# A first-layer product by seven block products instead of eight, beside an FFT convolution

## The chip, the cores and the metric

The kernel runs on one core of a Trainium2 chip, as one program. The time is the device time of an execution in microseconds (us); three executions of the kernel before took 1133.19, 1133.28 and 1133.93 us, median 1133.28.

An execution is worked on by TensorE (PE, matmuls, with PEld for the loading of their stationary operands), VectorE (DVE), ScalarE (ACT), GpSimd (POOL), SyncE (SP) and 16 DMA engines. Matmuls here write to tiles in PSUM, which the kernel divides into eight banks of 512 fp32 columns; the other operands lie in SBUF. Each engine works through its instructions in the order in which the built program has them, and waits on semaphores for the others.

## The reference

The input x has 2048 tokens of 576 channels. After a layer norm the result is the sum of three things: x itself, a state-space layer, and a dense layer.

```python
xn = (x - mean) / sqrt(var + 1e-5)
K  = real(sum over n of C[d,n] * exp(dt*A[d,n]*l) * dt*B[d,n])        # l = 0..2047, n = 0..127
y  = causal convolution of xn with K by FFT, + xn * Dskip
h  = silu(xn @ w1)            # w1: 576 x 4608
out = x + y + h @ w2          # w2: 4608 x 576
```

All inputs and the output are fp32.

## The kernel before, in words

**Precision.** The matmuls work in the type fp32r; the kernel's constants for it are cut to 12 bits of significand. Nearly every operand a is split into a high part (a cast on ScalarE, `gh`, `w1h`, `kh`) and a low part (a subtraction on VectorE, `gl`, `w1l`, `kl`), and a product is three matmuls: high x high, high x low, low x high.

**The dense layer** (`ffn`). The hidden 4608 features are 36 tiles of 128, in nine chunks of four (`FT`, `NCH`). The tokens are two halves of 1024, and each half two blocks of 512. For a block and a feature tile `up` (L276) writes a bank `ph` [128 features, 512 tokens]: 576 channels are four full slices of 128 and a rest of 64, so there are 3 x 4 matmuls for the slices and two for the rest, whose high and low parts lie one over the other in the 128 rows. That is 14 matmuls of 512 columns. SiLU, cast and subtraction (L292 to L294) make `gh` and `gl`. `down` (L296) then takes 128 tokens at a time, and for each half of the 576 output channels runs 12 matmuls of 288 columns into a bank `po` and adds it to `acc` on VectorE. The main loop (L343) goes over half, chunk and block; it puts the next block's four `up` between the four `down` of the present one. `load_w1` fetches the w1 columns of two feature tiles at once, `split_w1` and `split_w2` make high and low parts.

**The convolution** runs beside it. First come layer norm and transposes; then a generator (`kgen`) builds K in tables on VectorE and ScalarE, a first FFT stage (`kp`, `z` on TensorE, `spread` for the input) writes `d1k` and `d1u` to DRAM; then 32 rounds of the spectral stage (`spectral`, L632) load a slab of each (`kr`, `ur`), split it (`kh`, `kl`, `uh`, `ul`), transform it with the matrices `mm` (`pk`, `pu`), multiply (copies `ka`, `kb` by ScalarE out of `pk`, three products on VectorE and a sum `y`), split `y` (`yh`, `yl`), transform back (`pb`) and write the copy `yo` to `d2`. Round k+1's front stands ahead of round k's `pb`. At the end `tail` loads `d2` again (`ys`, L724) and `add_conv` (L731) adds the last transform `py` to the output rows: for the first token half into rows read back from DRAM (`r0`), for the second into `acc`.

**What sets the order.** `weave` (L31) advances the generator of the dense layer, and at each of its 288 steps lets the side generator go on as far as the step it names; `marks` and `tail_at` (L755) are such places as shares of all steps. A scheduler then moves instructions among the engines' queues by its own estimates; `tc.high_priority` and `behind` (an issue order between two instructions) steer it. PSUM: pool `ps1` has two banks (`ph`), `ps2` three (`po`), `pss` three for all side work.

## Time and profile before

| | |
|---|---|
| median of three executions | 1133.28 us (1133.19 to 1133.93) |
| span of the profiled execution, first to last instruction | 1133.7 us |
| its own time as a run | not listed; the slowest of the three is 0.2 us above its span, the median 0.4 below |
| TensorE busy | 1112.3 us, 9184 matmuls |
| VectorE busy | 916.6 us |
| ScalarE busy | 711.7 us |
| granted TensorE clock, mean | 0.997 |
| spectral stage, first to last `pb` | 697.2 to 1018.9 us |

How to read the rows that follow. Slices: the span in 40 equal parts, one digit each, the busy share in tenths. Windows: a stretch, its length, then the busy time and the number of instructions of each engine. Groups: line, engine, operation, output and inputs by the program's names (with shape), how many, then busy time in all, mean nanoseconds of one, and the idle time of the engine just before, with what ended it. Timeline: start, duration, engine, line, operation. An end of a matmul is modelled, and matmuls overlap: the distance between starts tells what one costs.

### The profile page before, as it was taken

How to read it: one execution, taken by the hardware profiler on the slowest of the kernel's cores; microseconds unless marked ns; L12 is line 12 of the kernel's file. 1: busy time of each engine (PE TensorE's matmuls, PEld its weight loads, DVE VectorE, ACT ScalarE, POOL GpSimd, SP SyncE). 2: the span in 40 equal slices, each digit the busy share in tenths (PEclk: the TensorE clock that was granted, in tenths of full speed). 3: DMA queues.
4: the chain of work that ended last, by engine and by line, in shares of the span. 5: the costliest groups of instructions: out<-in, count | busy, mean ns of one | idle time of the engine just before them, and what ended most of it. 6: DMA issues, size and time to landing. Idle time of an engine off the chain costs nothing.

```text
span 1133.7 us, 22905 instructions
## 1 busy us (share of the span) xinstructions
PE 1112.3 (98%) x9184; PEld 1002.8 (88%) x9184; DVE 916.6 (81%) x1540; ACT 711.7 (63%) x1235; POOL 74.4 (7%) x130
## 2 busy tenths in 40 slices
PE   6999999999999999999989999999999999999998
...
DVE  6699898999999999999979838787777778763433
ACT  4665456666767676667666647777777877752211
...
GB/s 271 136 158 201 146 34 82 82 92 103 91 97 65 137 69 119 53 163 169 263 116 103 77 160 143 155 178 125 159 131 151 150 136 184 82 101 193 231 174 56
DMA packets 160458, 151.24 MB, mean 133 GB/s; under 512 B 87216, under 2 KB 127168, under 8 KB 159712
## 3 DMA queue, kind: packets, MB, share of 16 engines
...
q10 hardware_dynamic: 384, 0.89, 0.3%
...
## 4 chain that ended last, share of the span: by engine, by line
PE 81%; DVE 11%; DMA 3%; ACT 2%; issue 2%; POOL 0%; SPq 0%; ACTq 0%; DVEq 0%
PE po L309 35%; PE ph L284 28%; PE kp L598 3%; PE ph L286 2%; PE ph L285 2%; PE pk L721 2%; PE pu L721 2%; PE pb L721 2%; PE z L613 1%; PE py L741 1%; DMA dxt<-xt 1%; DVE gl L294 1%; DVE S L577 1%; DMA w2r<-in_B_w_dram 1%; DVE w2l L273 1%
## 5 line engine op out<-in xcount | busy, mean ns | idle before, releaser
L309 PE MATMUL po<-w2h,gh 128*128 128x288 f32 x1152 | 339.1, 298 | 6.3 <-ACT gh L293 3.2
L309 PE MATMUL po<-w2l,gh 128*128 128x288 f32 x1152 | 338.0, 295 | 0.0
L309 PE MATMUL po<-w2h,gl 128*128 128x288 f32 x1152 | 334.6, 296 | 0.5 <-DVE gl L294 0.4
L309 PEld LDWEIGHTS po<-w2h,gh 128*128 128x128 f32 x1152 | 215.8, 188 | 18.2 <-issue 4.2
L309 PEld LDWEIGHTS po<-w2l,gh 128*128 128x128 f32 x1152 | 216.3, 188 | 4.3
L309 PEld LDWEIGHTS po<-w2h,gl 128*128 128x128 f32 x1152 | 215.1, 188 | 3.4 <-DVE gl L294 1.0
L284 PE MATMUL ph<-xh,w1h 128*128 128x512 f32 (+1 forms) x592 | 162.1, 390 | 0.7 <-ACT xh L122 0.7
L284 PE MATMUL ph<-xl,w1h 128*128 128x512 f32 (+1 forms) x592 | 162.2, 390 | 0.0
L284 PE MATMUL ph<-xh,w1l 128*128 128x512 f32 (+1 forms) x592 | 161.7, 387 | 0.0
L313 DVE TENSOR_TENSOR acc<-po,acc 128x288 f32<-128x288 f32 x288 | 126.5, 452 | 37.2 <-PE po L309 35.5
L292 ACT ACTIVATE gf<-ph 128x512 f32<-128x512 f32 (+1 forms) x148 | 86.8, 587 | 104.0 <-PE ph L286 94.9
L294 DVE TENSOR_TENSOR gl<-gf,gh 128x512 fp32r<-128x512 f32 (+1 forms) x148 | 99.4, 673 | 48.4 <-ACT gh L293 47.8
L284 PEld LDWEIGHTS ph<-xl,w1h 128*128 128x128 f32 x592 | 109.5, 191 | 21.5 <-issue 0.4
L284 PEld LDWEIGHTS ph<-xh,w1l 128*128 128x128 f32 x592 | 108.7, 190 | 19.9
L284 PEld LDWEIGHTS ph<-xh,w1h 128*128 128x128 f32 x592 | 104.8, 190 | 18.6 <-issue 2.3
L293 ACT CAST gh<-gf 128x512 fp32r<-128x512 f32 (+1 forms) x148 | 89.9, 609 | 17.9 <-PE po L309 15.2
L557 ACT ACTIVATE c<-th,magic 128x1040 f32<-128x1040 f32 x36 | 42.1, 1169 | 52.4 <-DVE C L578 30.1
L271 ACT CAST w2h<-w2r 128x576 fp32r<-128x576 f32 x72 | 47.2, 673 | 29.6 <-DMA w2r<-in_B_w_dram 17.4
L559 ACT ACTIVATE c<-th 128x1040 f32<-128x1040 f32 x36 | 38.7, 1074 | 36.0 <-DVE th L558 36.0
L273 DVE TENSOR_TENSOR w2l<-w2r,w2h 128x576 fp32r<-128x576 f32 x72 | 53.6, 752 | 6.2 <-ACT w2h L271 6.1
L255 DVE TENSOR_TENSOR w1l<-w1r,w1h 128x640 fp32r<-128x640 f32 x72 | 56.9, 820 | 1.0 <-ACT w1h L253 0.8
L577 DVE TENSOR_TENSOR S<-th,C 128x1024 f32<-128x1024 f32 x36 | 43.9, 1220 | 16.8 <-ACT th L560 16.8
...
## 6 DMA issues: line engine op xcount, KB each, us to landing
w2r<-in_B_w_dram SPq DMA_DIRECT2D x72, 288.0 KB, 3.3
w1r<-in_B_w_dram SPq DMA_DIRECT2D x35, 512.0 KB, 3.8
d1u<-u POOLq DMA_DIRECT2D x32, 288.0 KB, 2.7
d1k<-stage SPq DMA_DIRECT2D x18, 512.0 KB, 6.8
ur<-d1u SPq DMA_DIRECT2D x32, 288.0 KB, 3.9
kr<-d1k SPq DMA_DIRECT2D x32, 288.0 KB, 2.7
d<-yo POOLq DMA_DIRECT2D x32, 288.0 KB, 3.9
ys<-d SPq DMA_DIRECT2D x32, 288.0 KB, 9.2
```

The costliest lines, as they stand in the source:

```text
L255: pins["w1l"] = nc.vector.tensor_sub(l1, src, h1).ins
L271: pins["w2h"] = nc.scalar.copy(h2, r2).ins
L273: nc.vector.tensor_sub(l2, r2, h2)
L284: nc.tensor.matmul(ph, w[:, kt, :], v[:, kt, a:e], start=n + kt == 0, stop=False)
L292: nc.scalar.activation(gf, ph, AF.Silu)
L293: pins["gh"] = nc.scalar.copy(gh, gf).ins
L294: pins["gl"] = nc.vector.tensor_sub(gl, gf, gh).ins
L309: pins["pe"] = nc.tensor.matmul(po[:, :HD], G[blk, t][g][:, js], W2[half, c, t][w][:, hs], start=n == 0, stop=n == 3 * FT - 1).ins
L313: nc.vector.tensor_add(acc[j][:, hs], po[:, :HD], acc[j][:, hs])
L557: nc.scalar.activation(c65, th, AF.Identity, bias=magic)
L577: nc.vector.tensor_mul(ov3, t[:, :, 0:64].rearrange("n d (x y) -> n d x y", y=32), mv3)
L721: nc.tensor.matmul(dst, st, mv[:, hs], start=n == 0, stop=n == 3 * len(terms) - 1)
```

## The change

Seven of the nine chunks in the second token half (`WINO_C = 2` and on) compute the first product in another way. Take a pair of feature tiles (256 features), the two blocks of the half (1024 tokens) and the 512 channels of the full slices: w1 is a 2 x 2 matrix of blocks (two feature tiles, two halves of 256 channels), x likewise (two halves of channels, two blocks of tokens). Strassen's method in Winograd's form needs seven block products instead of eight, of sums of blocks. The rest of 64 channels is added as before.

- `wino_x` makes the sums of x once per half (S1 to S4, from the high and low parts), and `d4`, a difference for the rest of the channels.
- `sums` makes the sums of w1 for each pair on VectorE; `prep` and `split` make the high and low parts of what is used: `c1` and `c2` from w1 itself, `t13` and `t24` from the sums.
- Per pair, `wino_ffn` runs the products into four banks: `pb` (from `ps2`), in which three of them and a last one build up, `pf` (from `pss`), and the two `ps1` banks, `pa` and `pc`, which are held all the time. A copy of `pb` into `pa` and one of `pf` to SBUF (`f5`) are made by ScalarE; `pc` = `pb` + `f5` and `f5` = `pb` + `f5` are sums on VectorE, written where the next product goes on adding. `gate` is SiLU and the split; for `f5` it reads SBUF.
- `down` takes a list of terms: blocks of one pair or of two pairs in a row, always four rows of 128 tokens at a time.
- To make room, the pool of the spectral stage (`kl`) has one buffer of everything but the matrices, of which there are two of one round each (before: two of two rounds each); `y2` goes and `kb` is written over; the tail has four `ys` and two `r0` buffers, and loads a row's `ys` behind the `add_conv` four rows earlier. The dense layer has 276 steps, and the marks are counted anew.

The diff, cut to its core:

```diff
@@ -64,6 +64,7 @@
     nc = tc.nc
     FT = 4
     NCH = NFT // FT
+    WINO_C = 2
...
@@ -293,21 +295,22 @@
                 pins["gh"] = nc.scalar.copy(gh, gf).ins
                 pins["gl"] = nc.vector.tensor_sub(gl, gf, gh).ins
 
-        def down(blk, jj):
+        def down(blk, jj, terms=None):
             half, c, b = blk
             j = 8 * half + 4 * b + jj
             js = slice(jj * P, (jj + 1) * P)
             if half == 1 and c == NCH - 1:
+                add_conv(j, acc[j])
                 conv_load(j + AHEAD)
-                add_conv(j, acc[j])
+            terms = terms or [(G[blk, t], W2[half, c, t]) for t in range(FT)]
             for h in range(2):
                 hs = slice(h * HD, (h + 1) * HD)
                 po = ps2.tile([P, 512], F32, tag="ps2", name="po")
                 n = 0
-                for t in range(FT):
+                for gs, ws in terms:
                     for g, w in ((0, 0), (0, 1), (1, 0)):
-                        pins["pe"] = nc.tensor.matmul(po[:, :HD], G[blk, t][g][:, js], W2[half, c, t][w][:, hs],
-                                                      start=n == 0, stop=n == 3 * FT - 1).ins
+                        pins["pe"] = nc.tensor.matmul(po[:, :HD], gs[g][:, js], ws[w][:, hs],
+                                                      start=n == 0, stop=n == 3 * len(terms) - 1).ins
                         n += 1
...
-        for i, blk in enumerate(blocks):
+        plain = blocks[:2 * (NCH + WINO_C)]
+        for i, blk in enumerate(plain[:-1]):
             half, c, b = blk
-            later = i + 1 < len(blocks)
+            later = True
             new = (half, c + 1) if c + 1 < NCH else (half + 1, 0)
-            more = new[0] < 2
+            more = new < (1, WINO_C)
...
+                if new == (1, WINO_C) and (b, step) == (0, "u2"):
+                    load_w1(1, WINO_C, 0)
+        yield from wino_ffn(load_w1, load_w2, split_w2, R1, W2, plain[-1], down)
+
+    def wino_ffn(load_w1, load_w2, split_w2, R1, W2, before, down):
+
+        ps_a = ps1.tile([P, 512], F32, tag="ps1", name="pa")
+        ps_c = ps1.tile([P, 512], F32, tag="ps1", name="pc")
+        A, A22, S1, S2, S3, S4, x40, x41, d4 = wino["x"]
+        for t in (ps_a, ps_c):
+            nc.tensor.matmul(t, x40[:, :P], x40, start=True, stop=True)
+        G, WT = {}, {}
+
+        def split(src, name, n):
+            h = wp.tile([P, 5, P], F32R, tag="w1h", name="w1h", bufs=FT + 1)
+            l = wp.tile([P, 5, P], F32R, tag="w1l", name="w1l", bufs=FT + 1)
+            k = src.shape[1]
+            with behind(pins["gh"]):
+                nc.scalar.copy(h[:, :k], src)
+            nc.vector.tensor_sub(l[:, :k], src, h[:, :k])
+            WT[name, n] = h, l
+
+        def raw(n):
+            return R1[1, n // 2, n % 2 * 2]
+
+        def sums(n):
+            r1 = raw(n)
+            tr = [wino["pool"].tile([P, 4, P], F32, tag="tr", name="tr", bufs=2) for _ in range(2)]
+            nc.vector.tensor_sub(tr[0].rearrange("p (l k) f -> p l k f", l=2),
+                                 r1[:, 0:4, P:2 * P].rearrange("p (l k) f -> p l k f", l=2),
+                                 r1[:, 0:2, :].rearrange("p k (l f) -> p l k f", l=2))
+            nc.vector.tensor_add(tr[1][:, 0:2], tr[0][:, 2:4], r1[:, 0:2, 0:P])
+            nc.vector.tensor_sub(tr[1][:, 2:4], r1[:, 2:4, 0:P], tr[1][:, 0:2])
+            WT["raw", n] = tr
+
+        def prep(n, part):
+            if n >= NFT // 2:
+                return
+            r1 = raw(n)
+            if part == "c1":
+                split(r1[:, 0:5, 0:P], "c1", n)
+            elif part == "c2":
+                split(r1[:, 2:5, P:2 * P], "c2", n)
+            elif part == "t13":
+                split(WT["raw", n][0], "t13", n)
+            elif part == "t24":
+                split(WT["raw", n][1], "t24", n)
+
...
+        def prod(dst, w, x, start=False, stop=False):
+            (wh, wl), (xh, xl) = w, x
+            n = 0
+            for a, v in ((wh, xh), (wh, xl), (wl, xh)):
+                for kt in range(2):
+                    pins["pe"] = nc.tensor.matmul(dst, a[:, kt], v[:, kt], start=start and n == 0, stop=stop and n == 5,
+                                                  skip_group_check=True).ins
+                    n += 1
+
+        def rest(dst, name, n, at, x4, stop=True):
+            for i in range(2):
+                pins["pe"] = nc.tensor.matmul(dst, WT[name, n][i][:, at], x4, start=False, stop=stop and i == 1,
+                                              skip_group_check=True).ins
+
...
+        first, end = WINO_C * FT // 2, NFT // 2
+
...
+        def downs(n):
+
+            if n < first:
+                return [lambda jj=jj: down(before, jj) for jj in range(4)]
+            b = 1 - n % 2
+            if n == first:
+                ns = (n,)
+            else:
+                ns = (n - 1, n)
+            return run_of(b, ns)
+
+        def run_of(b, ns):
+            fs = [2 * n + i for n in ns for i in range(2)]
+            blk = (1, NCH - 1 if ns[-1] == end - 1 else WINO_C, b)
+            return [lambda jj=jj: down(blk, jj, [(G[b, f], W2[1, f // FT, f % FT]) for f in fs]) for jj in range(4)]
+
+        for n in range(first, end):
+            d = downs(n - 1)
+            pb = ps2.tile([P, 512], F32, tag="ps2", name="pb2")
+            pf = pss.tile([P, 512], F32, tag="pss", name="pf")
+            f5 = wino["pool"].tile([P, 512], F32, tag="f5", name="f5", bufs=1)
+            prod(pb, unit("c1", n, 0), A[0], start=True)
+            with tc.high_priority():
+                nc.scalar.copy(ps_a, pb)
+            prod(pf, unit("t13", n, 0), S1, start=True)
+            rest(pf, "c2", n, 2, x41)
+            with tc.high_priority():
+                nc.scalar.copy(f5, pf)
+            yield 0
+            d[0]()
+            second(n, 0, "split")
+            second(n, 1, "split")
+            yield 0
+            prod(pb, unit("t24", n, 0), S2)
+            with tc.high_priority():
+                nc.vector.tensor_add(ps_c, pb, f5)
+            d[1]()
+            second(n + 1, 0, "load")
+            second(n + 1, 1, "load")
+            if n + 1 < end:
+                sums(n + 1)
+            prep(n + 1, "c1")
+            yield 0
+            prod(pb, unit("t13", n, 2), S3)
+            with tc.high_priority():
+                nc.vector.tensor_add(f5, pb, f5)
+            d[2]()
+            prep(n + 1, "t13")
+            yield 0
+            d[3]()
+            yield 0
+            gate(f5, 1, 2 * n + 1)
+            prod(ps_c, unit("c2", n, 0), S4)
+            rest(ps_c, "c2", n, 2, d4)
+            gate(ps_c, 0, 2 * n + 1)
+            prep(n + 1, "c2")
+            prod(ps_a, unit("c1", n, 2), A[1])
+            rest(ps_a, "c1", n, 4, x40)
+            gate(ps_a, 0, 2 * n)
+            yield 0
+            prod(pb, unit("t24", n, 2), A22)
+            rest(pb, "c1", n, 4, x41)
+            gate(pb, 1, 2 * n)
+            prep(n + 1, "t24")
+            load(n + 2)
+            yield 0
+        b = 1 - (end - 1) % 2
+        for f in run_of(b, (end - 2, end - 1)):
+            f()
+            yield 0
+        for k, f in enumerate(run_of(1 - b, (end - 1,))):
+            f()
+            if k % 2:
+                yield 0
+
+    def wino_x(sx, xp):
+
+        (ah, al, x40), (bh, bl, x41) = xts[2], xts[3]
+
...
+        e = sx.tile([P, 512], F32, name="e4")
+        e2 = sx.tile([P, 512], F32, name="e42")
+        d4 = xp.tile([P, 512], F32R, name="d4")
+        x21, x22 = join(bh, bl, 0, "x21"), join(bh, bl, 2, "x22")
+        nc.vector.tensor_add(x22, x21, x22)
+        S1 = parts(x22, *new("s1"))
+        x11 = join(ah, al, 0, "x11")
+        nc.vector.tensor_sub(x21, x11, x21)
+        nc.vector.tensor_sub(x11, x22, x11)
+        S2 = parts(x11, *new("s2"))
+        x12 = join(ah, al, 2, "x12")
+        nc.vector.tensor_sub(x12, x12, x11)
+        S4 = parts(x12, *new("s4"))
+        nc.vector.tensor_sub(e, x40.bitcast(F32), x41.bitcast(F32))
+        nc.scalar.copy(e2[:64], e[64:])
+        nc.vector.tensor_add(e[:64], e[:64], e2[:64])
+        nc.scalar.copy(d4[:64], e[:64])
+        nc.vector.tensor_sub(d4[64:], e[:64], d4[:64])
+        yield 0
+        S3 = parts(x21, bh[:, 0:2], bl[:, 0:2])
+        wino["x"] = ([(ah[:, 0:2], al[:, 0:2]), (ah[:, 2:4], al[:, 2:4])], (bh[:, 2:4], bl[:, 2:4]),
+                     S1, S2, S3, S4, x40, x41, d4)
+        wino["pool"] = xp
 
     kl = yp = pa = tail_at = None
     kf = {}
@@ -631,16 +845,12 @@
 
     def spectral():
         def front(k):
-            if k % 2 == 0:
-                mm = kl.tile([P, 2, 4, P], F32R, tag="mm", name="mm")
-                nc.gpsimd.dma_start(mm, cm23[:, k:k + 2])
-                mats.append(mm)
-            mk = mats[-1][:, k % 2]
+            mk = kl.tile([P, 4, P], F32R, tag="mm", name="mm", bufs=2)
+            nc.gpsimd.dma_start(mk, cm23[:, k])
             us, ks = load_split(d1u[k * P:(k + 1) * P, :], "u"), load_split(d1k[k * P:(k + 1) * P, :], "k")
             ka = kl.tile([P, D], F32, tag="ka", name="ka")
-            kb = kl.tile([P, D], F32, tag="kb", name="kb", bufs=1)
-            y = kl.tile([P, D], F32, tag="y", name="y", bufs=1)
-            y2 = kl.tile([P, D], F32, tag="y2", name="y2", bufs=1)
+            kb = kl.tile([P, D], F32, tag="kb", name="kb")
+            y = kl.tile([P, D], F32, tag="y", name="y")
             for h in range(2):
                 hs = slice(h * HD, (h + 1) * HD)
                 pk = pss.tile([P, 512], F32, tag="pss", name="pk")
@@ -652,12 +862,11 @@
                 pu = pss.tile([P, 512], F32, tag="pss", name="pu2")
                 mm3(pu[:, :HD], [(mk[:, 0], mk[:, 1], us)], hs)
                 nc.vector.tensor_mul(y[:, hs], pu[:, :HD], ka[:, hs])
-                nc.vector.tensor_mul(y2[:64, hs], pu[64:, :HD], kb[:64, hs])
-                nc.vector.tensor_mul(y2[64:, hs], pu[:64, :HD], kb[64:, hs])
-            nc.vector.tensor_add(y, y, y2)
+                nc.vector.tensor_mul(kb[:64, hs], pu[64:, :HD], kb[:64, hs])
+                nc.vector.tensor_mul(kb[64:, hs], pu[:64, :HD], kb[64:, hs])
+            nc.vector.tensor_add(y, y, kb)
             return mk, split_of(y, "y")
 
-        mats = []
         nxt = front(0)
         for k in range(32):
             mk, ys = nxt
@@ -672,25 +881,25 @@
             nc.gpsimd.dma_start(d2.rearrange("(p k) d -> k p d", k=32)[k], yo)
             yield 1 + (k + 1) / 32
 
-    AHEAD = 6
+    AHEAD = 4
 
...
         def load_r0(j):
-            r0s[j] = yp.tile([P, 2, D], F32, tag="r0", name="r0", bufs=4)
+            r0s[j] = yp.tile([P, 2, D], F32, tag="r0", name="r0", bufs=2)
             nc.sync.dma_start(r0s[j], dr0[j * P:(j + 2) * P, :].rearrange("(i p) d -> p i d", p=P))
 
         def last(j):
-            conv_load(j + AHEAD, 8)
             add_conv(j, r0s[j - j % 2][:, j % 2, :])
+            conv_load(j + AHEAD)
             if j % 2:
                 store(r0s[j - 1], j - 1, (nc.gpsimd,))
 
         steps, at = [], tail_at[0]
         for j in range(8):
-            for f in (conv_load, load_r0)[:2 - j % 2]:
+            for f in (conv_load, load_r0)[j >= AHEAD:2 - j % 2]:
                 steps.append((at, f, j))
                 at += tail_at[1]
...
-    def conv_load(j, first=0):
-        if first <= j < NJ:
-            yss[j] = yp.tile([P, 4, HD], F32, tag="ys", name="ys", bufs=AHEAD + 2)
+    def conv_load(j):
+        if j < NJ:
+            yss[j] = yp.tile([P, 4, HD], F32, tag="ys", name="ys", bufs=AHEAD)
...
-        marks = (0.13, 0.595, 0.822)
-        tail_at = (0.895, 0.0045, 0.922, 0.005)
+        marks = (0.1357, 0.613, 0.855)
+        tail_at = (0.895, 0.0055, 0.919, 0.0052)
...
+        xp = ctx.enter_context(tc.tile_pool(name="xp", bufs=1))
+        with tc.tile_pool(name="sx", bufs=1) as sx:
+            for _ in wino_x(sx, xp):
+                yield 0.6215
+        with tc.tile_pool(name="kl", bufs=1) as kl:
             for at in spectral():
-                yield marks[1] + (at - 1) * (marks[2] - marks[1])
+                yield 0.6215 + (at - 1) * (marks[2] - 0.6215)
...
-    weave(fg, 2 * NCH * 2 * (FT + 4), sd)
+    weave(fg, 276, sd)
```

38 lines of the change are left out of this document (37 added, 1 removed).

## The prediction, made before the changed kernel had run

> **What bounds the kernel now.** I read the page first: span, busy shares, slices.
>
> ```profile
> span 1133.7 us, 22905 instructions
> PE 1112.3 (98%) x9184; PEld 1002.8 (88%) x9184; DVE 916.6 (81%) x1540; ACT 711.7 (63%) x1235; POOL 74.4 (7%) x130
> PE   6999999999999999999989999999999999999998
> DVE  6699898999999999999979838787777778763433
> ACT  4665456666767676667666647777777877752211
> ```
>
> TensorE is the bound nearly everywhere. VectorE is as full as TensorE in slices 7 to 20 (the generator of the convolution kernel) and at 70 to 80% in slices 24 to 35 (the spectral stage); both side engines are light in the last 100 us. A busy share hides pauses between matmuls, so next come two stages by windows, and the timeline for the distance from one matmul to the next.
>
> ```profile
> 200.00:500.00 300.00, 299.47 (x3165) 270.21 (x3164) 289.33 (x426) 205.16 (x310) 11.38 (x21) 1.00 0.37 94
> ...
> 1020.00:1134.00 114.00, 109.35 (x831) 89.24 (x829) 42.88 (x88) 22.59 (x38) 11.27 (x23) 1.00 0.64 163
> ```
> ```profile
> 660.00:1010.00 350.00, 349.97 (x2198) 324.25 (x2197) 268.74 (x488) 263.22 (x546) 25.89 (x47) 1.00 0.49 148
> ```
> ```profile
> 889.80 0.39 PE L285 MATMUL ph<-x,w1h 128*128 128x512 f32 x1
> 890.03 0.40 PE L286 MATMUL ph<-x,w1l 128*128 128x512 f32 x1
> ...
> 901.17 0.29 PE L309 MATMUL po<-w2l,gh 128*128 128x288 f32 x1
> 901.30 0.29 PE L721 MATMUL pu<-uh,mm 128*128 128x288 f32 x1
> ```
>
> Columns of the windows after the length: TensorE, weight load, VectorE, ScalarE, GpSimd, granted clock, DMA share, GB/s. A 512-wide matmul costs 0.23 us (0.227 in runs of them), a 288-wide one 0.13. In the spectral stage VectorE has 81 us to spare of 350 and ScalarE 87; TensorE has none.
>
> **The change, part by part.** *TensorE.* Call the two feature tiles of one first-weight load a pair; 14 pairs change. A pair had four outputs of 14 matmuls, 56; it gets seven products of 6 and four remainders of 2, 50. So 84 matmuls of 512 go, 2 come (they set up the two held banks): 82 x 0.227 = 18.6 us less. The down products, the spectral matmuls and the tail keep their number.
>
> *What the products cost elsewhere.* The durations come from the rows of the spectral stage and two of the whole span:
>
> ```profile
> L313 DVE TENSOR_TENSOR acc<-po,acc 128x288 f32<-128x288 f32 x84 | 37.6, 454 | 2.0 <-PE po L309 1.0
> L294 DVE TENSOR_TENSOR gl<-gf,gh 128x512 fp32r<-128x512 f32 x44 | 30.3, 690 | 20.0 <-ACT gh L293 19.6
> ...
> L654 DVE TENSOR_TENSOR y<-pu,ka 128x288 f32<-128x288 f32 x63 | 28.6, 454 | 12.0 <-ACT ka L649 8.9 <-PE pu L721 2.1
> ...
> L708 DVE TENSOR_TENSOR kl<-kr,kh 128x576 fp32r<-128x576 f32 x32 | 24.2, 758 | 31.4 <-ACT kh L707 31.3
> ...
> L657 DVE TENSOR_TENSOR y<-y,y 128x576 f32<-128x576 f32 x31 | 23.3, 752 | 0.0
> L255 DVE TENSOR_TENSOR w1l<-w1r,w1h 128x640 fp32r<-128x640 f32 x24 | 19.1, 821 | 0.2
> L273 DVE TENSOR_TENSOR w2l<-w2r,w2h 128x576 fp32r<-128x576 f32 x21 | 15.6, 753 | 0.1
> ```
> ```profile
> L293 ACT CAST gh<-gf 128x512 fp32r<-128x512 f32 x44 | 27.3, 620 | 0.9
> L292 ACT ACTIVATE gf<-ph 128x512 f32<-128x512 f32 x44 | 26.4, 599 | 12.3 <-PE ph L286 11.9
> L650 ACT ACTIVATE kb<-pk 64x288 f32<-64x288 f32 x64 | 26.1, 408 | 1.4 <-DVE y L656 0.3
> ...
> L648 ACT COPY ka<-pk 64x288 f32<-64x288 f32 x64 | 25.1, 392 | 11.6 <-PE pk L721 10.6
> ...
> L671 ACT COPY yo<-pb 128x288 f32<-128x288 f32 x60 | 23.1, 399 | 7.4 <-PE pb L721 6.4
> L707 ACT CAST kh<-kr 128x576 fp32r<-128x576 f32 x32 | 21.6, 674 | 1.9 <-DMA kr<-d1k 1.0
> ...
> L253 ACT CAST w1h<-w1r 128x640 fp32r<-128x640 f32 x24 | 16.2, 724 | 0.0
> L271 ACT CAST w2h<-w2r 128x576 fp32r<-128x576 f32 x21 | 13.7, 671 | 0.5 <-DMA w2r<-in_B_w_dram 0.2 <-PE po L309 0.2
> L621 ACT COPY stage<-z 128x512 f32<-128x512 f32 x2 | 1.1, 635 | 3.9 <-PE z L613 3.9
> ```
> ```profile
> L577 DVE TENSOR_TENSOR S<-th,C 128x1024 f32<-128x1024 f32 x36 | 43.9, 1220 | 16.8 <-ACT th L560 16.8
> ...
> L294 DVE TENSOR_TENSOR gl<-gf,gh 128x256 fp32r<-128x256 f32 x8 | 3.3, 415 | 2.2 <-ACT gh L293 2.2
> ```
>
> VectorE, per pair: splits 0.82 + 0.55 (384 wide, between the rows) + 2 x 0.69 in place of 2 x 0.82, +1.1; weight sums 0.69 + 2 x 0.42 = 1.5; two sums of products 1.4. That is 4.0, and 56 over 14 pairs. Once: a dozen 1024-wide operations on the tokens, 14.6 and some 2 for the small ones; 8 more additions into acc, 3.6. Together 76 us. ScalarE: per pair +1.0 of splits and two 512-wide copies, 1.2, and 4 casts once: some 37 us. Eleven VectorE rows of the stage (L313 to L273) sum to 283.7 where the window has 268.7 busy, thirteen ScalarE rows (L293 to L621) to 273.4 against 263.2, since one row overlaps the next: factors 0.947 and 0.963.
>
> *Where it lands.* The built order of the changed kernel, weighed with these rows, packs the spectral stage tighter: from its first to its last pb product TensorE has 277.6 us of matmuls instead of 321.5, VectorE 294 of row time instead of 266, ScalarE 273 instead of 255. With the factors that is 278, 278 and 263: three full engines. The order repeats every seven spectral rounds (two pairs); row time per round:
>
> ```
> round       1     2     3     4     5     6     7    sum
> TensorE    7.4   6.8   8.6  11.1  14.2   9.2   7.8  65.1
> VectorE    5.7   9.7  11.4   7.7  10.3  13.9   8.3  67.0
> ScalarE    6.0  10.8  10.5   6.6   8.5  12.8   6.7  61.9
> ```
>
> In rounds 1 to 3 ScalarE needs 27.3 x 0.963 = 26.3 us where TensorE has 22.8; in 4 to 7 TensorE has 42.3 and the others less. TensorE runs in order, so what it loses in the first three it does not get back. The least loss is 26.3 - 22.8 - 1.6 (ScalarE's copies of the next round can be that far ahead) = 1.9 per seven rounds. I walked the order by hand for more, from pb of round 1 at 0, with 0.40 for ka and kb copies, 0.65 for 576-wide operations and 0.1 for a hand-over: eight copies until 1.3, two casts and yo to 3.35, y sum on VectorE 3.4, yh 4.15, copy of pf 4.75, yl 4.95, sum into pc 5.6; only then may product t13 x S3 start, at 5.7 where the order has 3.7. ScalarE then works without a break from 4.75 to 13.55 and waits for product c1 x A1, ends its SiLU at 15.6, yh 16.25, copy of pb 16.85, gh 17.45, then ka and kb of the next round to 19.65. Only that frees the bank (three in this pool) for the second pu: 19.75 against 13.7. Later sums in the same seven add up to 2.5. I take 6.0; ends 1.9 and 8.5. There are 31/7 = 4.43 such groups: 26.6 us (8.4 to 37.7).
>
> *The start of the stage.*
>
> ```profile
> L598 PE MATMUL kp<-S x1152: 219/219/219, 169.3 to 655.6; 128*32 128x64 f32 x192
> ```
> ```profile
> L721 PE MATMUL pb<-yh,mm x128: 288/294/302, 697.2 to 1018.9; 128*128 128x288 f32 x128
> ...
> L708 DVE TENSOR_TENSOR yl<-y,yh x32: 747/759/761, 693.8 to 1014.4; 128x576 fp32r<-128x576 f32 x32
> ```
>
> Between the generator's last table and the first yl VectorE had 23 us of row time and 38 us of clock; it now has 39.2 x 0.947 = 37.1, and yl itself, 0.8, before pb may use it. The order gives TensorE 33.5 from the last kp to that pb: 4.4 late, with one hand-over 4.7 (2 to 8).
>
> *Smaller things.* The pair's pb holds one of three banks of the down products, two where pairs meet; an evacuation of 0.45 then stands between two halves in some places: 0 to 8 us over 14 pairs, I take 2, near the low end, since 0.45 is what the row shows per place. Buffers of one in the spectral stage: kr is reloaded behind kl, 2.7 us and 1.4 of casting, inside every round. mm is loaded per round, 16 more issues on GpSimd, which is 7% busy.
>
> ```profile
> mm<-in_cm_dram POOLq DMA_DIRECT2D x16, 512.0 KB, 4.3
> ...
> kr<-d1k SPq DMA_DIRECT2D x32, 288.0 KB, 2.7
> ```
>
> The tail's conv loads go from six ahead to four, issued behind add_conv instead of ahead of it. Their first py now stands 60 us of matmuls behind the last pb instead of 17, so I cost them at nothing. On SP's queue the loads of the last two rows stand behind the store of rows 8 and 9, which waits for the down product of row 9; the order leaves them 8.5 us from there to their py.
>
> ```profile
> DMA to landing us min/median/max: 4.0/9.2/13.0
> ```
>
> The lower end held when few loads were under way, as then; without that cover the end is up to 4 us later (0 to 4, I take 0). The moved marks are steps counted anew (276 for 288); the generator keeps its place.
>
> *Sum.* Against the profiled execution, span 1133.7, some 0.4 over the median of 1133.28 and 0.2 under the slowest run: 1133.7 - 18.6 + 26.6 + 4.7 + 2.0 - 0.4 = 1148.0.
>
> **A rule weighed.** TensorE's idle of 3.15 us was followed by a slow stretch:
>
> ```profile
> 575.00:580.00 5.00, 2.45 (x14) 1.98 (x12) 1.73 (x2) 4.09 (x6) 0.00 (x0) 1.00 0.76 224
> 580.00:585.00 5.00, 4.24 (x19) 4.01 (x20) 5.00 (x8) 4.14 (x10) 0.54 (x1) 0.66 0.00 1
> ```
> ```profile
> 580.60 0.40 PE L309 MATMUL po<-w2h,gh 128*128 128x288 f32 x1 [3.15 <-ACT gh L293]
> ```
>
> 5 x (1 - 0.66) = 1.7 us were lost beside the idle itself. My walk has one idle of 4 us per seven rounds (15.7 to 19.75); if each were followed by that loss, 4.43 x 1.7 = 7.5 more, 1155.5. The Trainium skill, TensorE: Matmul & The Clock Gate, "Why this matters for your kernels", warns of idle gaps over about 3 us between bursts of matmuls, which put the array back to half rate; by that rule the time would be this 1155.5, and the row agrees with it once.
>
> **Rivals.** *The gain survives:* ScalarE keeps just its least loss, 8.4, and the start costs 2: 1133.3 - 18.6 + 8.4 + 2 = 1125. It decides if the loss of a group is under 3 us. For it: VectorE ran 289 of 300 us in the generator while TensorE lost 0.5. Against it: there TensorE waited for no chain through ScalarE. At the best 1115. *The matrix load sets the rounds:* mm of round k+2 overwrites that of k, so its load starts behind pb of k, and the order has the first pk of k+2 just 1.8, 1.8, 2.5, 5.0, 5.9, 3.2 and 4.6 us later. With 4.4 for a load that is 8.3 per group; if half comes on top, 1148 + 18 = 1166, if all, 1185. Against it: half the bytes, and pk waits for kl as late. *The clock gate* above: 1155.5. That the matmuls do not go away is excluded by the order.
>
> **Chances.** Two tenths of a per cent, about what a measurement tells here, is 2.3 us. Forecast without the clock loss 0.35 and with it 0.17, matrix load 0.13: slower 0.65. Gain survives 0.31. In between 0.04. The likeliest case alone has 1133.3 - 18.6 + (8.4 to 37.7) + (2 to 8) + (0 to 8), in practice 1137 to 1160; the range, to leave out a tenth on each side, is 1121 to 1170.
>
> **What would show it.** Right: the products and remainders together 700 matmuls where the pairs had 784; idle TensorE in the spectral stage of some 27 us, ended by ScalarE (ka, kb) and VectorE in the first rounds of each seven, with VectorE over 90% there; about 5 us before the first pb; nothing in the last 100 us. Wrong: a spectral stage without TensorE idle (then 1115 to 1125), pk waiting for mm above all, or a new wait for ys in the tail.

## The result: 1204 us, and the profile after

The changed kernel takes 1204.01 us (four runs, 1201.54 to 1205.23) where the kernel before takes 1133.61 (four runs, 1133.19 to 1134.53): a ratio of 1.0612, 95% interval 1.0595 to 1.0628. The forecast was 1148; the direction came out, the loss is 70 us where 14 were forecast. The profiled execution took 1201.54 us with a span of 1199.8, 66.1 more than the span before.

The page of the changed kernel, its busy shares and slices:

```profile
span 1199.8 us, 23093 instructions
PE 1126.0 (94%) x9102; PEld 993.5 (83%) x9102; DVE 984.0 (82%) x1661; ACT 739.9 (62%) x1297; POOL 81.2 (7%) x146
PE   6999999999999999999999878979889898999898
DVE  6799999999999999999995868878788788746444
ACT  4665556666666776766764368687677876634120
PEclk9999999999999999999999879999999999999899
```

The matmuls did go away: 9102 for 9184. But TensorE pauses from slice 23 on, and over a slice neither VectorE nor ScalarE is full there (no digit over 8). The same in windows (length, TensorE, weight load, VectorE, ScalarE, GpSimd, granted clock, DMA share, GB/s), first the start of the stage, the spectral stage and the rest of the changed kernel, then the stage of the kernel before:

```profile
640.00:706.00 66.00, 54.99 (x415) 46.30 (x413) 44.19 (x69) 27.45 (x48) 2.01 (x3) 0.87 0.29 74
706.00:1044.00 338.00, 299.96 (x1772) 261.81 (x1772) 273.32 (x507) 253.29 (x539) 33.12 (x61) 0.99 0.45 134
1044.00:1199.00 155.00, 147.81 (x1054) 123.74 (x1052) 74.79 (x147) 41.21 (x72) 11.22 (x23) 0.97 0.51 136
```
```profile
698.00:1019.00 321.00, 321.00 (x2037) 298.92 (x2037) 251.60 (x459) 241.12 (x505) 24.43 (x45) 1.00 0.46 140
```

TensorE, which never paused in the stage before, is idle for 38 of 338 us now, 11 of the 66 before it, 7 behind it. The clock, 1.00 before, is 0.87, 0.99 and 0.97: 66 x 0.13 + 338 x 0.01 + 155 x 0.03 = 17 us at the most. That counts slow time in which TensorE stood still as well. Four stretches in which the clock is 0.50 (671.74 to 678.57, 695.63 to 709.28, 798.03 to 801.44 and 1118.88 to 1125.71 us) hold 24.8 us of TensorE's work; half of that, 12.4 us, is what the clock cost, where the kernel before lost 3.3 in the same way. Three rows of groups give the places by which I cut the time (last table product `kp`, first and last `pb` of the rounds, last `py`):

```profile
L812 PE MATMUL kp<-S x1152: 219/219/219, 168.1 to 650.9; 128*32 128x64 f32 x192
L930 PE MATMUL pb<-yh,mm x128: 288/295/606, 705.2 to 1043.2; 128*128 128x288 f32 x128
L950 PE MATMUL py<-ys,s x256: 402/427/686, 1103.8 to 1193.3; 64*32 64x288 f32 x128
```

The built order, weighed with 0.228 and 0.133 us per matmul, says what these stretches cost without a pause; what the chip took beyond that is lost. Last matmul means the last of all, 1129.1 and 1195.2 us.

| us: order, chip, lost | kp to first pb | first to last pb | last pb to last matmul |
|---|---|---|---|
| before | 40.1, 41.6, 1.5 | 322.1, 321.7, -0.4 | 100.7, 110.2, 9.5 |
| changed | 33.4, 54.3, 20.9 | 278.1, 338.0, 59.9 | 133.1, 152.0, 18.9 |

So 19.4 more is lost at the start, 60.3 in the stage and 9.4 behind it, 89.1 in all. Against that stand 18.7 of matmuls saved and 4.4 by which the stretch up to the last `kp` became shorter than its matmuls explain (650.9 us for 655.6; 0.3 of the 4.7 are matmuls): 89.1 - 18.7 - 4.4 = 66.0, the whole difference.

Who TensorE waited for (total, times, longest):

```profile
PE pk L930 <- DMA mm<-in_cm_dram: 19.3, 12, 2.5
PE pt L122 <- DVE xn L190: 8.9, 1, 8.9
PE pu L930 <- ACT kb L861: 5.6, 10, 1.3
PE po L312 <- DVE gl L447: 5.4, 5, 1.3
PE pb L930 <- ACT kb L861: 3.9, 9, 0.5
PE py L950 <- DMA ys<-d: 3.6, 1, 3.6
```

The second row is at the very start of the program and was there before. The first is the rival called the matrix load; `pu` on `kb` is the wait that the forecast named; `py` on `ys` was costed at nothing. One round shows the first of them, in the timeline (start, duration, engine):

```profile
706.61 0.44 PE L930 MATMUL pb<-yh,mm 128*128 128x288 f32 x1
...
707.35 0.55 POOL L849 DMA_DIRECT2D mm<-in_cm_dram  x1 [16.29 <-PE pb L930]
...
709.75 0.40 PE L436 MATMUL pf<-x,w1l 128*128 128x512 f32 x1
...
711.64 0.37 PE L930 MATMUL pk<-kh,mm 128*128 128x288 f32 x1 [1.49 <-DMA mm<-in_cm_dram]
```

The load can be issued only when `pb` has let go of the tile, at 707.35; `pk` starts 4.3 us later, with TensorE idle for the last 1.5.

### The profile page after: what moved, and what is told of

Same layout as the page of the kernel before. It is cut to its first block, busy times and chain, and to the rows that moved or that the text cites. A ratio compares the mean times of both kernels' runs of the same rounds, so it can differ in the third digit from the quotient of the medians.

```text
span 1199.8 us, 23093 instructions
## 1 busy us (share of the span) xinstructions
PE 1126.0 (94%) x9102; PEld 993.5 (83%) x9102; DVE 984.0 (82%) x1661; ACT 739.9 (62%) x1297; POOL 81.2 (7%) x146
## 4 chain that ended last, share of the span: by engine, by line
PE 51%; issue 24%; DVE 11%; DMA 6%; ACT 5%; POOL 2%; SPq 0%; POOLq 0%; DVEq 0%; ACTq 0%
PE po L312 24%; PE ph L286 14%; PE pb L430 2%; PE kp L812 2%; PE z L827 1%; DVE acc L316 1%; PE ph L287 1%; PE ph L288 1%; POOL d L881 1%; PE py L950 1%; POOL mm L849 1%; DMA dxt<-xt 1%; DMA mm<-in_cm_dram 1%; DMA w2r<-in_B_w_dram 1%; DMA ys<-d 1%
## 5 line engine op out<-in xcount | busy, mean ns | idle before, releaser
L286 PE MATMUL ph<-xh,w1h 128*128 128x512 f32 (+1 forms) x368 | 99.3, 387 | 0.6 <-ACT xh L123 0.6
L286 PE MATMUL ph<-xl,w1h 128*128 128x512 f32 (+1 forms) x368 | 98.8, 384 | 0.0
L286 PE MATMUL ph<-xh,w1l 128*128 128x512 f32 (+1 forms) x368 | 97.5, 382 | 0.0
L294 ACT ACTIVATE gf<-ph 128x512 f32<-128x512 f32 (+1 forms) x92 | 52.8, 575 | 44.0 <-PE ph L288 26.6
L286 PEld LDWEIGHTS ph<-xl,w1h 128*128 128x128 f32 x368 | 66.9, 190 | 12.4
L286 PEld LDWEIGHTS ph<-xh,w1l 128*128 128x128 f32 x368 | 66.6, 188 | 12.0
L286 PEld LDWEIGHTS ph<-xh,w1h 128*128 128x128 f32 x368 | 65.3, 191 | 10.6 <-ACT xh L123 0.9
L296 DVE TENSOR_TENSOR gl<-gf,gh 128x512 fp32r<-128x512 f32 (+1 forms) x92 | 60.6, 660 | 6.9 <-ACT gh L295 6.6
L930 PE MATMUL pk<-kh,mm 128*128 128x288 f32 x128 | 37.9, 312 | 25.3 <-DMA mm<-in_cm_dram 19.3
L295 ACT CAST gh<-gf 128x512 fp32r<-128x512 f32 (+1 forms) x92 | 55.3, 603 | 5.4 <-PE po L312 4.1
```

The source lines that it names most:

```text
L286: nc.tensor.matmul(ph, w[:, kt, :], v[:, kt, a:e], start=n + kt == 0, stop=False)
L294: nc.scalar.activation(gf, ph, AF.Silu)
L295: pins["gh"] = nc.scalar.copy(gh, gf).ins
L296: pins["gl"] = nc.vector.tensor_sub(gl, gf, gh).ins
L930: nc.tensor.matmul(dst, st, mv[:, hs], start=n == 0, stop=n == 3 * len(terms) - 1)
```

## The experiments

Theories. Products theory, the forecast's: the products fill ScalarE and VectorE between the rounds, and TensorE pauses at chains through them. Matrix theory: `mm` comes late. Buffer theory: single buffers hold each round behind the one ahead. Later ones are named where they come up. The kernel before, run beside each set, took 1134.1 to 1135.4 us (medians); the ratios are against it.

**1. The small buffers alone.**

```diff
 (kernel before)
-        with tc.tile_pool(name="kl", bufs=2) as kl:
+        with tc.tile_pool(name="kl", bufs=1) as kl:
 (spectral: as in the changed kernel, mm per round, no y2)
```

> The kernel before, with the spectral stage's buffers of the changed kernel (every tile once, the matrix loaded per round) and without the products; the tail is left as it was. Products theory (the products, packed between the rounds, fill ScalarE and VectorE, and TensorE pauses at chains through them): the buffers alone cost little, 1134 to 1140 us. Buffer theory (with one buffer each, a round can't start before the one ahead of it is done): most of the 60 us lost in the stage show here, 1160 to 1190. Matrix theory (the load of a round's matrix starts behind pb of two rounds ahead and comes late): a round has 10 us of matmuls here where the changed kernel has 8.9, so part of it shows, 1137 to 1150, with pk waiting for mm.

Measured: 1183.29 us, ratio 1.0423 (1.0397 to 1.0448). It looks like the buffer theory, and is not. The rows of `pb`, then the waits:

```profile
L716 PE MATMUL pb<-yh,mm x128: 288/294/606, 696.9 to 1097.5; 128*128 128x288 f32 x128
```
```profile
PE py L736 <- DMA ys<-d: 27.8, 7, 10.6
PE py L736 <- issue: 10.1, 1, 10.1
```

The scheduler, which sees the buffers too, drew the rounds apart: 396.9 us of matmuls in its order, 400.6 on the chip, 3.7 lost. The price is paid behind the stage, where the last transforms have no work left to stand beside (`py` waits 37.9 us, 10.1 of them for nothing that the profile shows). So the run says that small buffers change the order, and nothing on what they cost in the tight order.

**2. The matrix in two tiles.** One half serves `pk` and `pu`, the other `pb`.

```diff
-            mk = kl.tile([P, 4, P], F32R, tag="mm", name="mm", bufs=2)
-            nc.gpsimd.dma_start(mk, cm23[:, k])
+        def matrix(k, which):
+            if k < 32:
+                d, o, n = ((mats, 0, "mm"), (backs, 2, "m3"))[which]
+                d[k] = kl.tile([P, 2, P], F32R, tag=n, name=n, bufs=2)
+                nc.gpsimd.dma_start(d[k], cm23[:, k, o:o + 2])
...
             ys = nxt
+            matrix(k + 2, 0)
...
+            matrix(k + 2, 1)
             nc.gpsimd.dma_start(d2.rearrange("(p k) d -> k p d", k=32)[k], yo)
```

> The changed kernel with the matrix in two tiles of half the size, one for pk and pu, one for pb, in the same space; the first is free after pu, a round earlier than the whole was, and its load is issued a round earlier. Matrix theory: the 19.3 us in which pk waits for mm go, with the slow pitch behind them some 25: 1175 to 1185 us. Products theory: other waits take their place (kb, gl), 1190 to 1204. Buffer theory: 1190 to 1204.

Measured: 1176.76 us, ratio 1.0364 (1.034 to 1.0388), 27.3 less than the changed kernel. The scheduler's order is not the same, but about as tight: 276.9 us of matmuls in the stage for 278.1, and what its rounds fall short of 9 us sums to 36.6 for 35.0. No wait for the matrix is left in the list, and the stage takes 313.0 us:

```profile
L942 PE MATMUL pb<-yh,m x128: 288/295/609, 703.4 to 1016.4; 128*128 128x288 f32 x128
```
```profile
PE pu L942 <- ACT kb L860: 9.2, 7, 1.7
```

The matrix theory holds for 27 us; the stage still loses 36.1, and `pu` waiting for `kb`, the forecast's wait, is now the first in the stage.

**3. Products late, in six pairs.** `WINO_C = 6`, the stage's buffers as before, the token sums behind the stage.

```diff
-    WINO_C = 2
+    WINO_C = 6
...
-        with tc.tile_pool(name="kl", bufs=1) as kl:
+        with tc.tile_pool(name="kl", bufs=2) as kl:
             for at in spectral():
...
+        xp = ctx.enter_context(tc.tile_pool(name="xp", bufs=1))
+        with tc.tile_pool(name="sx", bufs=1) as sx:
+            for _ in wino_x(sx, xp):
+                yield 0.83
```

> Products only in the last three chunks of the second half (six pairs instead of fourteen), behind the spectral stage, which has the buffers of the kernel before; the tail is that of the changed kernel. The six pairs save 36 - 2 matmuls of 0.228 us, 7.8. Products, buffer and matrix theories all say that the spectral stage is as before; what is left is the setting up of the sums and the tail, together 2 to 12: 1128 to 1138 us. If the products cost by themselves, wherever they stand (6 us per pair as in the changed kernel), 1150 or more.

Measured: 1189.82 us, ratio 1.0483 (1.0455 to 1.0512). All theories missed. Windows of the stage's even part, of where it meets the products, and of the rest:

```profile
697.00:950.00 253.00, 251.47 (x1595) 233.37 (x1594) 201.37 (x369) 193.89 (x407) 20.01 (x37) 1.00 0.48 145
950.00:1020.00 70.00, 40.82 (x154) 31.30 (x152) 51.77 (x82) 40.40 (x84) 4.85 (x9) 0.61 0.25 79
1020.00:1185.00 165.00, 156.77 (x1098) 130.18 (x1098) 84.85 (x167) 49.43 (x87) 10.68 (x22) 1.00 0.49 131
```

The stage ran as before up to 950. Then the dense layer's plain part was used up, the scheduler put the last rounds one behind the other (2.9 us of matmuls between them on the mean of seven, 7.2 on the chip, at a clock of 0.61), and the products waited for the token sums (11.5 us for `s1h`), which can't begin before the stage's space is free. The four rounds with no matmuls beside them (2.4 us in the order) took 6.8 to 8.8 us: that became the floor theory.

**4. Without kb's copies.**

```diff
-                nc.scalar.mul(kb[:64, hs], pk[64:, :HD], -1.0)
-                nc.scalar.copy(kb[64:, hs], pk[64:, :HD])
...
-                nc.vector.tensor_mul(kb[:64, hs], pu[64:, :HD], kb[:64, hs])
-                nc.vector.tensor_mul(kb[64:, hs], pu[:64, :HD], kb[64:, hs])
+                nc.vector.tensor_mul(kb[:64, hs], pu[64:, :HD], ka[:64, hs])
+                nc.vector.tensor_mul(kb[64:, hs], pu[:64, :HD], ka[64:, hs])
```

> The changed kernel without the four copies per round from pk into kb (the two products of VectorE read ka in their place, so the convolution is not computed); all else stays. It takes 4 x 0.40 us of ScalarE out of each round, 51 us over the stage, and nothing from TensorE or VectorE. Products theory with ScalarE as the limit: 30 to 50 of the lost 60 us come back, 1155 to 1175 us. Matrix theory: the load is as late as before, 1190 to 1204. Buffer theory: a round's chain is shorter by 0.8 to 1.6 us, 1180 to 1195.

Measured: 1185.86 us, ratio 1.045 (1.0426 to 1.0475), 18.2 less than the changed kernel for 51 us of ScalarE less; `pk` still waits 20.1 us for the matrix. Fewer than the products theory asked: ScalarE has a part in the loss, not the whole. The time lies in the range of the buffer theory, which 9 tests.

**5. The rounds spread.** On the split matrix.

```diff
-        marks = (0.1357, 0.613, 0.855)
+        marks = (0.1357, 0.613, 0.893)
```

> The kernel with the split matrix, and the spectral stage's last mark moved from 0.855 to 0.893: its built order has 305 us of matmuls from the first pb product to the last instead of 277, taken from the 61 us between the last pb and the first py. Crowding theory (the rounds are packed tighter than VectorE, ScalarE and the round's own chain can follow; the split kernel took 313 us for them): 20 to 30 of the 36 us lost in the stage come back, 1147 to 1157 us. Pair theory (each pair of products costs its pauses wherever the rounds stand): nothing comes back, 1173 to 1181.

Measured: 1166.1 us, ratio 1.0273 (1.0249 to 1.0296), 10.7 less: between the two. The stage's loss fell from 36.1 to 23.8, and 13.5 of these 23.8 are in its first six rounds, whose order the mark did not move.

**6. Without the token sums.** On the split matrix.

```diff
 (wino_x)
-        e = sx.tile([P, 512], F32, name="e4")
-        ...
-        S3 = parts(x21, bh[:, 0:2], bl[:, 0:2])
+        S1 = S3 = S4 = (bh[:, 0:2], bl[:, 0:2])
+        S2 = (ah[:, 0:2], al[:, 0:2])
+        d4 = x40
```

> The kernel with the split matrix, without the sums of tokens and their splits at the start of the stage (the products read plain token tiles, so the feed-forward part of the second half is not computed); every matmul stays. Sums theory (some 17 us of VectorE work between the generator's last table and the first round set the 20 us lost there): the stretch from the last kp to the first pb falls from 53 to 35 to 41 us, 1160 to 1165 us. If the start is lost to single buffers or to the first loads: 1172 to 1178.

Measured: 1159.37 us, ratio 1.0213 (1.0192 to 1.0235), 17.4 less, nearly all at the start (53.0 to 37.5 us between `kp` and `pb`). The sums theory holds. The changed kernel's VectorE shows why these sums cost more than they take:

```profile
661.31 0.69 DVE L296 TENSOR_TENSOR gl<-gf,gh 128x512 fp32r<-128x512 f32 x1 [1.74 <-ACT gh L295]
664.71 3.50 DVE L548 TENSOR_TENSOR x<-xh,xl 128x1024 f32<-128x1024 f32 x3 [2.71 <-DMA d1k<-stage]
```

The last `kp` is at 650.9, but the sums stand in the generator's space and can't begin before its last store has landed, at 664.7. Windows of the same run show VectorE before and after that moment:

```profile
651.00:664.00 13.00, 12.54 (x90) 11.14 (x85) 3.61 (x7) 4.33 (x8) 0.00 (x0) 1.00 0.50 82
664.00:690.00 26.00, 21.25 (x112) 17.65 (x113) 25.20 (x35) 10.02 (x15) 0.94 (x2) 0.87 0.14 40
```

For 13 us it is nearly idle, then it is full for 26 while TensorE waits.

**7. Products last, in four pairs.** As 3, with `WINO_C = 7`, so that a plain chunk stands between the stage and the products.

```diff
-    WINO_C = 2
+    WINO_C = 7
...
+        yield 0.845
+        with tc.tile_pool(name="sx", bufs=1) as sx:
+            for _ in wino_x(sx, xp):
+                yield 0.88
```

> Products only in the last two chunks of the second half (four pairs), 16 steps behind the end of the spectral stage, which has the buffers of the kernel before; the tail is that of the changed kernel. The matmuls are 5.0 us shorter than before. Crowding theory (products cost next to nothing where the side engines are light): 1129 to 1136 us with 0 to 7 for the tail's fewer loads ahead. If a pair costs its pauses wherever it stands (some 3 us each): 1138 to 1146.

Measured: 1160.49 us, ratio 1.0224 (1.02 to 1.0249), outside both ranges. The stage lost 1.6 us (314.6 for 313.0), so the wide rounds held. But the scheduler drew the rounds over the chunk that I had meant to keep free (in its order the first product, which needs no sums, stands 12 us of matmuls ahead of the last `pb`), and the sums began when the last round's store let go of the space:

```profile
1017.16 4.63 DVE L548 TENSOR_TENSOR x<-xh,xl 128x1024 f32<-128x1024 f32 x4 [0.38 <-DMA d<-yo]
```

The first product with `s1h` waited 7.2 us and the next 2.3, and from 1013 to 1063 TensorE worked 36.6 us of 50 at a clock of 0.90. Wherever the products begin, their sums have to be done before.

**8 and 13. Less ScalarE or less VectorE in the tight rounds.** On the split matrix: 8 is the edit of 4; 13 is

```diff
-                nc.vector.tensor_mul(kb[:64, hs], pu[64:, :HD], kb[:64, hs])
-                nc.vector.tensor_mul(kb[64:, hs], pu[:64, :HD], kb[64:, hs])
```

> The kernel with the split matrix and without the four copies per round from pk into kb (VectorE reads ka in their place, so the convolution is not computed): 51 us of ScalarE less over the stage, the matrix no longer late. ScalarE theory: the 36 us still lost in the stage fall to under 15, 1150 to 1158 us. VectorE theory (it has about as much to do and keeps it all): 1165 to 1177.

> The kernel with the split matrix, without the four 64-row products per round of pu with kb on VectorE (kb is added as it was copied, so the convolution is not computed): 1.8 us of VectorE less per round, 56 over the stage, the same matmuls. Taking the same amount from ScalarE gave 15.5 us. If a round's 8 to 9 us are a chain through both engines: as much again or more, 1155 to 1163. If ScalarE alone sets them: 1172 to 1177.

Measured: 1161.28 us, ratio 1.023 (1.0208 to 1.0253), for 8, and 1167.58, ratio 1.0289 (1.0271 to 1.0307), for 13. 51 us of ScalarE gave 15.5 us, 56 us of VectorE gave 9.2. Each time lies between the two ranges of its run. Both count, ScalarE more; neither is the limit alone. The windows of the stage in 8 and in 13:

```profile
705.00:1001.00 296.00, 288.51 (x1746) 260.69 (x1746) 270.58 (x506) 199.69 (x417) 48.66 (x90) 0.98 0.53 153
```
```profile
706.00:1010.00 304.00, 290.21 (x1760) 264.64 (x1760) 218.50 (x385) 248.75 (x539) 48.76 (x90) 0.98 0.51 149
```

With VectorE 91% busy (270.6 of 296) TensorE paused less than with VectorE at 72% (218.5 of 304). Over the whole stage neither engine is at its limit in either run. That is a mean over wide and tight rounds, and it does not hold inside the tight ones, as "The floor in numbers" shows.

**9. Two buffers in the tight rounds.** In the space that 6 leaves.

```diff
-        with tc.tile_pool(name="kl", bufs=1) as kl:
+        with tc.tile_pool(name="kl", bufs=2) as kl:
...
-            kb = kl.tile([P, D], F32, tag="kb", name="kb")
-            y = kl.tile([P, D], F32, tag="y", name="y")
+            kb = kl.tile([P, D], F32, tag="kb", name="kb", bufs=1)
+            y = kl.tile([P, D], F32, tag="y", name="y", bufs=1)
```

> The kernel with the split matrix and without the sums, with the space that the sums leave used for two buffers of every tile of the spectral stage but y and kb; the order of TensorE is the same. Buffer theory (the 33 us still lost between the first and the last pb product come of a round that has to wait for the single buffers of the one ahead): they fall under 15, from 1159 to 1138 to 1146 us. Products theory (VectorE and ScalarE have no more time than the matmuls leave them, whatever the buffers): 28 to 33 stay, 1154 to 1160.

Measured: 1159.27 us, ratio 1.0214 (1.0199 to 1.0229), against 1159.37. The order of TensorE is not quite that of 6 (277.6 us of matmuls in the stage for 276.9), but the loss in the stage stays, 34.1 for 33.2. The buffer theory falls: with the matrix split, the other single buffers cost nothing that can be measured. The Trainium skill, Perfetto Trace Analysis, "Optimization Strategy", says that the same gap repeating for a stretch can mean that there is too little memory for the next tile; here a tile that was not free in time made the gap for the matrix, though two tiles in the same space were enough, and memory did not make the rest of it.

**10. The tail's loads earlier.** On the split matrix.

```diff
-        tail_at = (0.895, 0.0055, 0.919, 0.0052)
+        tail_at = (0.866, 0.0055, 0.919, 0.0052)
```

> The kernel with the split matrix, with the first four loads of the tail (ys) and r0 marked from 0.866 of the steps on instead of 0.895, some 30 us earlier and still behind the last round. If the 4.2 us in which py waits for ys, and the slow pitch behind them, come of these loads standing late on SP's queue behind the weights: 1169 to 1173 us against 1176.8. If four buffers are too few for any order of the loads: 1175 to 1179, with the wait at a later py.

Measured: 1172.15 us, ratio 1.0323 (1.0303 to 1.0342), 4.6 less. No `py` waits for `ys` any more, and the loss behind the last `pb` falls from 19.4 to 12.8. Four buffers were enough; the loads stood too late on SP's queue.

**11 and 12. Sums ahead, and even rounds.** An attempt to keep the gain: twelve pairs, so that one more plain chunk covers the sums; `x21` waits in two tiles that the products use later, and only S3 is split when they start; the rounds are spread up to 0.912 (11). Then they are marked evenly (12).

```diff
-    WINO_C = 2
+    WINO_C = 3
...
-        nc.vector.tensor_sub(x21, x11, x21)
+        keep = [xp.tile([P, 512], F32, tag=n, name="x21k", bufs=2) for n in ("gh2", "gl2")]
+        for k in range(2):
+            nc.vector.tensor_sub(keep[k], x11[:, k], x21[:, k])
...
-        marks = (0.1357, 0.613, 0.855)
-        tail_at = (0.895, 0.0055, 0.919, 0.0052)
+        marks = (0.1347, 0.6086, 0.912)
+        tail_at = (0.912, 0.0035, 0.919, 0.0052)
...
+                at = marks[1] + (at - 1) * (marks[2] - marks[1])
+                if at > 0.676 and sums:
+                    yield 0.676
+                    next(sums, None)
+                    sums = None
 (up to here 11 against the changed kernel; 12 against 11:)
-                at = marks[1] + (at - 1) * (marks[2] - marks[1])
+                at = 0.660 + (at - 1) * (0.912 - 0.660)
...
-        tail_at = (0.912, 0.0035, 0.919, 0.0052)
+        tail_at = (0.912, 0.0035, 0.932, 0.0052)
```

> An attempt at a faster version: the split matrix; products from the fourth chunk on (twelve pairs, 72 - 2 matmuls of 0.228 us less than before, 16.0), so that the sums of tokens are made beside one more plain chunk and only S3 is split where the products start; the rounds spread over 302 us of matmuls. If the loss at the start is the sums pressed between the generator and the first products, 15 of its 20 us go, and with the spread 1140 to 1150 us. If the start is lost to VectorE's total work, 1155 or more.

> The kernel with the sums ahead, its rounds marked from 0.660 to 0.912 of the steps instead of 0.609 to 0.912, and the tail's rows from 0.932; nothing else. In its built order the matmuls from one round's first pb to the next are rarely under 8 us; the shortfalls under 9 us per round sum to 11.7 us where the kernel with the sums ahead has 30.5 (and lost 34 us in the stage), the kernel with the split matrix 36.6 (lost 36), the kernel before 5.0 (lost none). Floor theory (a round takes 8 to 9 us on the chip whatever matmuls stand in it, and every round ordered tighter loses the rest): the loss falls by about 19, 1139 to 1146 us. If the 34 us were lost because the first products stand among those rounds: 1155 to 1163.

Measured: 1160.49 us, ratio 1.0227 (1.0212 to 1.0242), for 11. Its time is that of the second range, but the start did what the first one said: it lost 1 us (58.4 for 57.4 in the order). The spread failed: rounds right behind the first products were ordered 3.8, 2.4 and 2.4 us apart and took 5.6, 7.6 and 7.5. For 12, 1142.72 us, ratio 1.0070 (1.0052 to 1.0088): 17.8 less than 11, in the range of the floor theory. The loss in the stage fell by 12.3 (33.8 to 21.5), and that behind it, where the tail's rows were moved too, by 4.0. The start and the stage of 12:

```profile
651.00:709.00 58.00, 58.00 (x354) 52.55 (x354) 43.16 (x68) 31.61 (x56) 4.15 (x7) 1.00 0.43 107
709.00:1040.00 331.00, 320.50 (x1983) 291.85 (x1983) 286.17 (x536) 257.09 (x549) 48.10 (x89) 0.99 0.48 140
```

61 of the 70 us are back, with 16.0 of the 18.7 us of matmuls still saved; it is the best of the versions with products, and still 0.7% behind the kernel before.

**15 and 16. VectorE's work on GpSimd.** On 12: the three weight sums of a pair (15), or the addition of `kb` to `y` (16).

```diff
-            nc.vector.tensor_sub(tr[0].rearrange(
+            nc.gpsimd.tensor_sub(tr[0].rearrange(
 (and the two lines behind it)
-            nc.vector.tensor_add(y, y, kb)
+            nc.gpsimd.tensor_add(y, y, kb)
```

> The kernel with even rounds, with the three weight sums of each pair on GpSimd instead of VectorE (18 us of VectorE less over twelve pairs; the sums are made a pair ahead). If VectorE's fill sets the 21 us still lost in the stage: 1134 to 1139 us. If they are lost to each round's own chain, or GpSimd's operations take too long or slow VectorE: 1141 to 1150.

> The kernel with even rounds, with the addition of kb to y (0.75 us per round) on GpSimd: 23 us of VectorE less over the stage, but GpSimd's time and two hand-overs more in each round's chain. If VectorE's fill sets the loss: 1135 to 1140 us. If the chain does: 1143 to 1155.

Measured: 1142.42 us, ratio 1.0065 (1.0051 to 1.0079), for 15: no change. For 16, 1155.3 us, ratio 1.018 (1.0166 to 1.0194), 12.6 more. GpSimd's rows (line, operation, count, busy, mean ns) of 16 and of 15 (one of its three):

```profile
L870 POOL TENSOR_TENSOR y<-y,kb 128x576 f32<-128x576 f32 x32 | 59.7, 1865 | 61.1 <-DVE kb L869 60.9
```
```profile
L401 POOL TENSOR_TENSOR tr<-w1r 128x512 f32<-128x512 f32 x12 | 18.1, 1505 | 76.0 <-DMA w1r<-in_B_w_dram 46.9 <-DMA w2r<-in_B_w_dram 13.4 <-DVE kb L868 7.7
```

But neither run took time off VectorE. Its busy time in 12, 15 and 16, with 36 and 32 operations fewer in the last two:

```profile
PE 1106.6 (97%) x9114; PEld 990.5 (87%) x9114; DVE 974.6 (85%) x1649; ACT 733.2 (64%) x1290; POOL 98.3 (9%) x178
PE 1106.4 (97%) x9114; PEld 991.4 (87%) x9114; DVE 975.0 (85%) x1613; ACT 731.8 (64%) x1290; POOL 139.8 (12%) x214
PE 1109.0 (96%) x9114; PEld 991.0 (86%) x9114; DVE 979.9 (85%) x1617; ACT 734.4 (64%) x1290; POOL 158.0 (14%) x210
```

Operations of VectorE became longer where GpSimd worked beside them. The subtraction `ul` in 12 and in 16:

```profile
L933 DVE TENSOR_TENSOR ul<-ur,uh 128x576 fp32r<-128x576 f32 x32 | 24.1, 753 | 1.3 <-ACT uh L932 1.0
```
```profile
L933 DVE TENSOR_TENSOR ul<-ur,uh 128x576 fp32r<-128x576 f32 x32 | 40.1, 1254 | 1.6 <-ACT uh L932 1.3
```

So 15 and 16 leave open whether VectorE's fill or the chain sets the loss. What 16 shows is that a slower step in each round (1865 ns for the 752 of VectorE), together with the longer VectorE operations beside it, costs 12.6 us over 31 rounds.

**The floor in numbers.** Distance from one round's first `pb` to the next, mean over the rounds that the order puts less than 8 us apart, and over those at 9 us or more:

| | under 8: rounds, order, chip | 9 or more: rounds, order, chip |
|---|---|---|
| before | 1: 6.0, 6.0 | 26: 10.8, 10.8 |
| changed | 16: 7.0, 9.5 | 11: 11.6, 12.4 |
| 2, split matrix | 16: 6.7, 8.8 | 15: 11.0, 11.2 |
| 8, ScalarE less | 13: 6.5, 7.6 | 12: 11.3, 11.6 |
| 13, VectorE less | 9: 5.5, 7.4 | 17: 10.7, 11.1 |
| 9, no sums, two buffers | 10: 5.9, 8.3 | 17: 10.5, 11.1 |
| 12, even rounds | 5: 7.2, 8.7 | 20: 11.1, 11.4 |

Rounds ordered wide cost what the order says or a few tenths more (0.8 in the changed kernel). Rounds ordered tight take 8.3 to 9.5 us on the mean in the versions with products and whole rounds, 7.4 and 7.6 where work of a round is left out (13 and 8); TensorE, which runs in order, can't win the rest back. It is no fixed number: in 2, rounds ordered at 6.0 took 8.6 to 9.9, and two ordered at 7.2 took 7.1.

What fills a tight round shows in windows of its own (length, then TensorE, weight load, VectorE, ScalarE): one ordered at 6.8 us in the changed kernel, one at 4.2 in 2, one at 4.2 in 13, one at 5.8 in 8.

```profile
868.88:877.81 8.93, 7.09 (x42) 6.02 (x40) 8.19 (x15) 8.78 (x20) 1.09 (x2) 1.00 0.58 173
```
```profile
784.62:792.65 8.03, 5.34 (x29) 3.84 (x27) 7.75 (x15) 7.86 (x18) 2.17 (x4) 1.00 0.62 177
```
```profile
852.74:859.30 6.56, 4.50 (x28) 3.93 (x27) 5.22 (x9) 6.43 (x16) 1.62 (x3) 1.00 0.67 185
```
```profile
850.30:856.98 6.68, 6.23 (x39) 5.53 (x38) 6.24 (x12) 6.40 (x15) 1.62 (x3) 1.00 0.69 193
```

ScalarE is 98% busy in the first three (8.78 of 8.93, 7.86 of 8.03, 6.43 of 6.56) and 96% in the last, VectorE 92, 97, 80 and 93%. The other rounds of these kinds read much the same; one in 8, ordered at 4.2, took 6.0 with ScalarE 88% busy. So in these rounds ScalarE has no time left, though it is 75 to 82% busy over the stages of the changed kernel and of 13. That is the mechanism of the forecast, and the floor is in part the plain sum of ScalarE's work in the round. It is not the whole: the rounds without matmuls beside them in 3 took 6.8 to 8.8 us with ScalarE 56 to 86% busy. The runs do not part the two, since each edit also changed the order.

## Why the prediction was wrong, step by step

- *The matmuls*, 18.6 less: right, 82 fewer and 18.7 in the order.
- *The spectral stage*, 26.6 with ends 8.4 and 37.7: measured 60.3. The step that failed is that the sum held one mechanism, and the matrix load at nothing. That rival was real and ran beside it: 27.3 us were got back by the split (the rival's gaps of 8.3 us per group of seven rounds would have made 37). The argument against it, half the bytes and `kl` as late, did not hold: 12 waits end at the matrix. It should have been a term, not an alternative with 0.13. `pk` waiting for `mm` above all, and a new wait for `ys`, were the forecast's own signs of being wrong; both came.
- The walk by hand itself: 36.1 us are lost with the matrix split, 8.1 per group for the 6.0 that I took, inside its ends of 1.9 and 8.5. That sum holds slow clock and small waits too, so the agreement is rough. Mechanism and rounds were right in the main: the first three of each seven lose most (10.3, 8.9 and 11.8 on the chip for 7.4, 6.8 and 8.0, waits for the matrix included), and in the second of them ScalarE is 98% busy. VectorE over 90%, a sign named for all three, holds for that one alone. That it is ScalarE alone is not so (8 and 13). The table of row times per round, in which 6.8 us of TensorE stood beside 10.8 of ScalarE, could have been read as a floor per round at once.
- *The start*, 4.7 with ends 2 and 8: measured 19.4. The step compared VectorE's work with TensorE's over the whole stretch, as if both could begin at the last `kp`; the sums began 13.8 us later, when the generator's store had left their space. Experiment 6 gives 17.4 for the sums.
- *The banks of ps2*, 2.0: not measured by itself; the waits of `po` for `acc` sum to 1.5 us, so it is small.
- *The tail's loads*, costed at nothing, 0 to 4: 3.6 us of wait; that stretch lost 9.4 more than before, and 10 gives 4.6 to 6.6 of it to these loads. The cover that I named, 60 us of matmuls ahead of the first `py`, is there. The loads did not use it: `ys` of the later rows were issued from 1105 us on, behind weights.
- *The generator keeps its place*: it ended 4.7 us earlier, in my favour; why is open.
- *The clock*, a rival worth 7.5: 12.4 us by the stretches above, against 3.3 before (mean clock 0.986 and 0.997). It was no rival either, as it adds to what the waits cost, and part of each figure above is its work. The place was wrong: not one loss per group, but 6.8 + 13.7 us of slow clock around the start of the stage, 3.4 in the rest of it and 6.8 in the tail.
- *The gain survives*, 0.31: no. Its condition, under 3 us lost per group, was missed by far (59.9 / 4.43 = 13.5).

What stays open: the 21.5 us that the stage of 12 still loses, in rounds at 8 to 9 us and in single waits; how much of a tight round is ScalarE's and VectorE's work and how much their hand-overs; and whether a shorter round (fewer copies out of `pk`) would make the change pay.
